# Attention and two feed-forward layers: token order inside a tile by residue mod 4, plain heads permuted in the matrix product, merged copies of x

## The chip, the cores and the metric

One core of a Trainium2 chip. The metric is the device time of one execution in microseconds (us), lower is better; for the kernel before it is the median of three runs.

## The reference

```python
# q, k, v: (4, 8, 576, 64) fp32; heads 0-3 "plain", heads 4-7 "dilated"
scores = q @ k.T / 8
rel = pos[:, None] - pos[None, :]
mask_plain = (rel >= 0) & (rel < 32)
mask_dil   = (rel >= 0) & (rel < 128) & (rel % 4 == 0)
attn = softmax(where(mask, scores, -1e9)) @ v            # per batch and head
x = attn.transpose(0, 2, 1, 3).reshape(2304, 512)         # tokens x model
x = (silu(x @ w_gate) * (x @ w_val)) @ w_out              # 512 -> 1536 -> 512
h = x @ w_in                                              # 512 -> 2048
return (h - tanh(h)) @ w_out2                             # 2048 -> 512, fp32
```

## The kernel before

The 2304 tokens are cut into six tiles of 384 (`TT`). The kernel holds x, the attention output, transposed: for a tile, two buffers of 128 partitions (two heads of 64 dimensions each) with a high and a low half in fp32r, `x[tile][kc][:, s, hp % 2, token]`, s = 0 for high and 1 for low. The feed-forward products then run in three passes over these halves (`up`, L543, the first layer before its sums exist; `product`, L554, with seven products in place of eight; `ffn1_out` L821 and `ffn2_out` L841).

Attention works in 48 units: a batch b (4), a pair of heads hp (hp 0 and 1 plain, 2 and 3 dilated) and a third g of the 576 queries, so 192 queries in three blocks of 64. For the dilated heads the host has sorted the 576 positions by residue mod 4, 144 of each residue in a row, so that their mask is the same band as that of the plain heads. A unit goes through these steps, each by one engine: load of q and k (SP queue, L472) and of v (L437); scores, three products (TensorE, L443); masked row maxima (VectorE, L448, three); exponentials with row sums (ScalarE, L454, three); 1 / sum (VectorE, L493 and L494, for one or two units together); normalisation (GpSimd, L458); three transposes (TensorE, L464); copy of the transposed weights `at` out of PSUM (VectorE L468 or ScalarE L470, in turn); the products with v, called mix here (TensorE, L510, moving operand `at`, stationary operand v, six per unit); and the copies of the result into x: high half by ScalarE (`put_hi`, L523), then the low half, PSUM minus high half, by VectorE (`put_lo`, L526).

`mixes` takes three units at a time, puts two of them in one PSUM bank and one in another, and makes one pair of copies per unit and piece. `spans` gives the pieces: a plain unit is 192 tokens in a row in one tile, so one piece of 192 columns. A dilated unit holds rows of one or two residues; its tokens lie in the tile at every fourth column, so each piece is written with a step of four fp32 elements (16 bytes), and a unit's piece is 48 or 96 columns long, since batches and tiles overlap (576 against 384).

The order of all work is made ahead of time by a planner written in the file (`Plan.order`): each task has an engine, an estimated duration, a priority and the ring buffers it needs; an engine takes the ready task of the lowest priority number. Attention units have priorities 0.3 apart in the order of `first_tile`; feed-forward tasks are put between them as their tiles of x and their weights become ready. Constants such as `KEEP_T`, `AHEAD` and `SECOND` bend this order. On the chip each engine then runs its list in order. Matrix weights come through the same SP queue and are converted from fp64 bits by ScalarE and VectorE (L332 to L345, L314, L317). The last stage of layer two adds up into `acc` (VectorE, L730) and stores 128 tokens at a time to the output (SP, L854).

Of the kernel before, what the change touches and what calls it, by code (L numbers as in the profile page):

```python
# [21 lines left out]
P = 128  # L22
# [235 lines left out]
def attention_then_two_ffns(ctx, tc, qk, vt, masks, w1, w2, out):  # L258
# [130 lines left out]
    x_done = [([], []) for _ in range(NT)]  # L389
    x_of = [[[] for _ in range(KC)] for _ in range(NT)]  # L390

    def spans(b, hp, g):

        base = b * S
        if hp < NP // 2:
            i, o = divmod(base + UT * g, TT)
            yield i, slice(0, UT), lambda xt, s: xt[:, s, hp % 2, o:o + UT]
            return
        cut = ((base // TT + 1) * TT - base) // DIL
        for r in range(DIL):  # L400
            for a0, a1 in ((0, cut), (cut, SA)):
                c0, c1 = max(r * SA + a0, g * UT), min(r * SA + a1, g * UT + UT)
                if c0 < c1:
                    i, o = divmod(base + DIL * (c0 - r * SA), TT)
                    yield (i, slice(c0 - g * UT, c1 - g * UT),
                           lambda xt, s, o=o, r=r, n=DIL * (c1 - c0): xt[:, s, hp % 2, o:o + n].rearrange(
                               "p (a f) -> p f a", f=DIL)[:, r, :])

    def idle(ps):

# [88 lines left out]
    def mixes(fronts, prio):  # L499

        banks = [new_ps() for _ in fronts[::2]]

        def mix():
            for j, (_, v, at, _) in enumerate(fronts):
                pv = banks[j // 2]
                covered[pv.slot] = 0
                for i in range(UN):
                    for h2 in range(2):
                        c, o = P * i + D * h2, j % 2 * UT + QT * i
                        nc.tensor.matmul(pv()[D * h2:D * h2 + D, o:o + QT],  # L510
                                         lhsT=v()[:KT, c:c + D], rhs=at()[:, c:c + D], start=True, stop=True)

        a = add_att("PE", 0.35 + 0.35 * len(fronts), prio, mix, [d for f in fronts for d in f[3]],
                    banks + [t for f in fronts for t in f[1:3]])
        a.fresh = idle(banks[0])
        for j, ((b, hp, g), _, _, _) in enumerate(fronts):
            pv = banks[j // 2]
            for i, cols, dst in spans(b, hp, g):
                n = cols.stop - cols.start
                cols = slice(j % 2 * UT + cols.start, j % 2 * UT + cols.stop)  # L520

                def put_hi(xt=x[i][hp // 2], cols=cols, dst=dst, pv=pv):
                    nc.scalar.activation(out=dst(xt(), 0), in_=pv()[:, cols], func=AF.Copy)  # L523

                def put_lo(xt=x[i][hp // 2], cols=cols, dst=dst, pv=pv):
                    nc.vector.tensor_tensor(out=dst(xt(), 1), in0=pv()[:, cols], in1=dst(xt(), 0).bitcast(F32),  # L526
                                            op=ALU.subtract)

                h = add_att("ACT", 0.05 + n / 1200 if n == UT else 0.035 + n / 850, prio, put_hi, [a], [pv, x[i][hp // 2]])
                x_of[i][hp].append(add_att("DVE", 0.07 + n / 960 if n == UT else 0.06 + n / 545, prio, put_lo, [h], [pv, x[i][hp // 2]]))  # L530
                x_done[i][hp // 2].append(x_of[i][hp][-1])

    covered = {}

# [296 lines left out]
    def ffn2_out(ws, ys, t, first, last, prio, end=False, early=None):  # L831
        pieces = []
        cuts = [(s, 0, DM) for s in range(NS)]
        if end:
            cuts[-1:] = [(NS - 1, 0, DM // 2), (NS - 1, DM // 2, DM)]
        for s, c0, c1 in cuts:
            def mm(ps, start=True, s=s, c0=c0, c1=c1):
                n = 0
                for w, y in zip(ws, ys):
                    for a, bb in PASSES:  # L840
                        nc.tensor.matmul(ps()[:, :c1 - c0], lhsT=y[0]()[:, a, s * P:(s + 1) * P],  # L841
                                         rhs=w[1][0]()[:, bb, c0:c1], start=(n == 0), stop=(n == 3 * len(ws) - 1))
                        n += 1
                covered[ps.slot] = c1 - c0

            pieces.append((mm, s * DM + c0, s * DM + c1, MM * 4 * len(ws) * (c1 - c0) / DM,
                           [d for _, d in ys] + [w[1][1] for w in ws], [w[1][0] for w in ws] + [y for y, _ in ys]))
        r = add_up(2, t, pieces, first, last, prio, early)
        if last:
            at, puts = r  # L850
            for (s, c0, c1), a in zip(cuts, puts):
                def store(s=s, c0=c0, c1=c1):
                    r0 = t * TT + s * P
                    nc.sync.dma_start(out=out[r0:r0 + P, c0:c1], in_=at()[:, s * DM + c0:s * DM + c1])  # L854

                plan.add("DMA", ISSUE, -1e6, store, [a], [at], work=0.9 * (c1 - c0) / DM)

# [105 lines left out]
    def first_tile(unit):  # L963
        b, hp, g = unit
        i = max(i for i, _, _ in spans(b, hp, g)) if hp < NP // 2 else b * S // TT
        return i, b, (hp < NP // 2) != PLAIN_FIRST, hp, g

    units = [(b, hp, g) for b in range(B) for hp in range(NP) for g in range(S // UT)]
    fronts, parts = [], []
    for n, unit in enumerate(sorted(units, key=first_tile)):  # L970
        prio = ATT0 + ATT_STEP * n
        if not parts:
            sm = new_sm()
        parts.append(attention(*unit, prio, ("DVE", "ACT")[n % 2], sm, len(parts)))
        many = FEW if n < SOON else TOGETHER
        if len(parts) == (1 if n < ALONE else ONE_SUM) or len(fronts) + len(parts) == many:
            fronts += inverted(parts, sm, prio - AHEAD)
            parts = []
        if len(fronts) == many:
            mixes(fronts, prio)  # L980
            fronts = []

    def given(*homes):
        got = {}
# [137 lines left out]
    def any_size():  # L1122
# [38 lines left out]

        for t in range(NT):
            xt = tile_of(t)
            rows = out[t * TT:(t + 1) * TT, :].rearrange("(s p) c -> p s c", p=P)
            for k in range(NK2):
                weights(wi, w2[k][:, :512])
                weights(wo, w2[k][:, 512:])
                h = ps[0][:, :TT]
                for kc in range(KC):
                    for n, (a, b) in enumerate(PASSES):  # L1170
                        nc.tensor.matmul(h, lhsT=wi[:, a, kc * P:(kc + 1) * P], rhs=xt[kc // 2][:, b, kc % 2, :],
                                         start=(kc == n == 0), stop=(kc == KC - 1 and n == 2))
                nc.scalar.activation(out=sq, in_=h, func=AF.Square)
                nc.scalar.activation(out=th, in_=h, func=AF.Tanh)
                nc.vector.scalar_tensor_tensor(out=g, in0=h, scalar=C2, in1=sq, op0=ALU.mult, op1=ALU.mult)
                nc.vector.tensor_tensor(out=th, in0=h, in1=th, op=ALU.subtract)
# [11 lines left out]
                part = at.rearrange("p (s c) -> p s c", s=NS)  # L1188
                if k == 0:
                    nc.sync.dma_start(out=rows, in_=part)  # L1190
                else:
                    nc.gpsimd.dma_start(out=rows, in_=part, accum_op=ALU.add)

    with tc.manual_schedule():
        for t in plan.order():
# [53 lines left out]
```

## Time and profile before

| | |
|---|---|
| median of three runs | 877.51 us (877.45 to 878.17) |
| the profiled execution, its own time | 877.31 us |
| its span, first to last instruction | 875.4 us |
| TensorE busy, share of the span | 863.8 us, 99% |
| VectorE | 722.1 us, 82% |
| ScalarE | 585.0 us, 67% |
| mean granted TensorE clock | 0.998 |

Time and span are of one execution; the 1.9 us between them lie outside the instructions. Matrix products are pipelined: a product's recorded duration reaches into the next one, so a TensorE that is busy all the time may still start its products later than it could. Every fp32 product stands in the trace as two records (288 for the 144 score products, 576 for the 288 mix products), every fp32r product as one.

### The profile page before, as it was taken

The numbers are of one execution on the slowest core, as the hardware profiler recorded it, in microseconds if no ns is written. First come the engines' busy times: TensorE is split into PE (matmuls) and PEld (weight loads), VectorE is DVE, ScalarE is ACT, GpSimd is POOL, SyncE is SP. The second block draws the span as 40 slices with busy tenths as digits, with TensorE's granted clock in tenths as the row PEclk, the third lists the DMA queues.
The fourth block names the chain that finished last, engine by engine and source line by source line (L and its number), as shares of the span: only waits on it lengthen the run. The fifth ranks groups of instructions, "written<-read, shape, count | busy, mean of one in ns | idle before, by whom it ended". The sixth has DMA issues, their size and how long they took to land.

```text
span 875.4 us, 15267 instructions
## 1 busy us (share of the span) xinstructions
PE 863.8 (99%) x5240; PEld 814.6 (93%) x5240; DVE 722.1 (82%) x1708; ACT 585.0 (67%) x1516; POOL 86.0 (10%) x116
## 2 busy tenths in 40 slices
PE   8999999999999999999999999999999999999996
PEld 6898999999999999999999999889989889898995
DVE  5999999989788788788759999978878777765675
ACT  6999757668667567668648887756666556564530
POOL 2333100000000000000000000011011010111100
PEclk9999999999999999999999999999999999999999
DMA  9997272583885885888895556899989796958995
GB/s 326 370 317 270 60 263 94 231 280 103 229 240 109 229 232 118 228 229 224 268 325 192 205 191 233 288 255 279 206 230 207 188 248 165 227 133 199 246 298 213
DMA packets 50455, 195.84 MB, mean 224 GB/s; under 512 B 5600, under 2 KB 12224, under 8 KB 50368
## 3 DMA queue, kind: packets, MB, share of 16 engines
q1 hardware_dynamic: 41728, 147.59, 47.0%
q0 software_dynamic: 8640, 47.19, 29.0%
q8 instruction: 43, 0.70, 0.3%
q14 instruction: 44, 0.36, 0.1%
HBM read 121.62 MB, written 73.14 MB: 222 GB/s over the span
## 4 chain that ended last, share of the span: by engine, by line
PE 88%; DVE 7%; DMA 1%; ACT 1%; issue 1%; POOL 0%; SPq 0%; POOLq 0%; DVEq 0%
PE ps L554 54%; PE ps L841 21%; PE ps L821 6%; PE ps L543 3%; PE ps L443 2%; PE ps L510 1%; DVE x L905 1%; DMA q<-qk 1%; PE ps L464 1%; DVE e L448 1%; DVE x L526 1%; DVE acc L920 1%; ACT e L454 1%; DVE t L701 0%; DVE t L698 0%
## 5 line engine op out<-in xcount | busy, mean ns | idle before, releaser
L554 PE MATMUL ps<-x,wc 128*128 128x384 f32 x2316 | 426.4, 336 | 0.0
L554 PEld LDWEIGHTS ps<-x,wc 128*128 128x128 f32 x2316 | 407.5, 188 | 4.4
L841 PE MATMUL ps<-wc,y 128*128 128x512 f32 (+1 forms) x870 | 208.9, 392 | 0.2 <-DVE t L701 0.2
L841 PEld LDWEIGHTS ps<-wc,y 128*128 128x128 f32 x870 | 161.9, 188 | 33.5 <-DVE t L701 0.6
L734 ACT ACTIVATE acc<-ps 128x512 f32<-128x512 f32 (+1 forms) x134 | 75.0, 560 | 77.4 <-PE ps L841 61.0
L761 POOL DMA_DIRECT2D sum<-acc x60 | 53.0, 883 | 678.4 <-ACT acc L734 273.2
L633 DVE TENSOR_TENSOR y<-t,y 128x384 fp32r<-128x384 f32 x168 | 92.4, 553 | 26.3 <-ACT y L630 26.0
L630 ACT ACTIVATE y<-t 128x384 fp32r<-128x384 f32 x168 | 86.4, 518 | 22.4 <-DVE t L701 8.4
L565 ACT ACTIVATE ps<-ps 128x384 f32<-128x384 f32 x156 | 73.7, 476 | 25.8 <-PE ps L554 22.1
L314 ACT ACTIVATE wc<-u 128x512 fp32r<-128x512 f32 x108 | 67.5, 631 | 26.6 <-PE ps L554 18.7
L317 DVE TENSOR_TENSOR wc<-u,wc 128x512 fp32r<-128x512 f32 x108 | 73.1, 684 | 3.7 <-ACT wc L314 2.4
L600 DVE TENSOR_TENSOR ps<-ps,t 128x384 f32<-128x384 f32 x56 | 31.5, 563 | 43.1 <-PE ps L554 43.1
L821 PE MATMUL ps<-y,wc 128*128 128x384 f32 x336 | 62.8, 337 | 0.0
L698 DVE SCALAR_TENSOR_TENSOR t<-t 128x384 f32<-128x384 f32 x96 | 52.7, 551 | 10.3 <-ACT t L695 9.5
L821 PEld LDWEIGHTS ps<-y,wc 128*128 128x128 f32 x336 | 58.8, 188 | 0.1
L454 ACT ACTIVATE e<-e,nm 128x96 f32<-128x96 f32 x144 | 52.1, 369 | 6.4 <-DVE nm L448 6.3
L695 ACT ACTIVATE t<-ps 128x384 f32<-128x384 f32 x72 | 34.9, 485 | 25.9 <-DVE ps L600 15.7
L332 ACT ACTIVATE u<-st 128x512 f32<-128x512 f32 x68 | 44.9, 666 | 9.0 <-DMA st<-w 8.7
L345 DVE SCALAR_TENSOR_TENSOR u<-st,u 128x512 uint32<-128x512 uint32 x68 | 46.8, 689 | 0.4
L340 DVE SCALAR_TENSOR_TENSOR u<-st,u 128x512 uint32<-128x512 uint32 x68 | 46.5, 684 | 0.7 <-DVE nm L448 0.2
L554 PE MATMUL ps<-y,wc 128*128 128x384 f32 x198 | 45.3, 336 | 0.0
L554 PE MATMUL ps<-ym,wm 128*128 128x384 f32 x198 | 43.0, 337 | 0.0
(87 smaller groups left out, 1077.2 us busy)
## 6 DMA issues: line engine op xcount, KB each, us to landing
x<-part SPq DMA_DIRECT2D x66, 768.0 KB, 7.2
sum<-acc POOLq DMA_DIRECT2D x60, 768.0 KB, 8.9
st<-w SPq DMA_DIRECT2D x68, 512.0 KB, 5.7
q<-qk SPq DMA_DIRECT2D x48, 304.0 KB, 5.4
sum<-acc SPq DMA_DIRECT2D x12, 768.0 KB, 5.8
part<-x SPq DMA_DIRECT2D x12, 768.0 KB, 3.4
acc<-sum SPq DMA_DIRECT2D x12, 768.0 KB, 7.5
v<-vt SPq DMA_DIRECT2D x47, 192.0 KB, 5.1
```

The source lines that it names most:

```text
L314: nc.scalar.activation(out=w()[:, 0, :], in_=u(), func=AF.Copy)
L317: nc.vector.tensor_tensor(out=w()[:, 1, :], in0=u(), in1=w()[:, 0, :].bitcast(F32), op=ALU.subtract)
L454: nc.scalar.activation(out=e()[:, i, :], in_=e()[:, i, :], func=AF.Exp, scale=-1.0, bias=nm()[:, i:i + 1], accum_out=sm()[:, sums.start + ...
L554: nc.tensor.matmul(ps()[:, :TT], lhsT=w()[:, i, c:c + P], rhs=rhs, start=(start and n == 0), stop=(n == 3 * len(cols) - 1), skip_group_che ...
L565: nc.scalar.activation(out=ps()[:, :TT], in_=src()[:, :TT], func=AF.Copy)
L630: nc.scalar.activation(out=y()[:, 0, :], in_=s(), func=AF.Copy)
L633: nc.vector.tensor_tensor(out=y()[:, 1, :], in0=s(), in1=y()[:, 0, :].bitcast(F32), op=ALU.subtract)
L698: nc.vector.scalar_tensor_tensor(out=sq(), in0=sq(), scalar=E0 / E1, in1=sq(), op0=ALU.add, op1=ALU.mult)
L734: nc.scalar.activation(out=o, in_=ps()[:, :c1 - c0], func=AF.Copy)
L761: nc.gpsimd.dma_start(out=keep, in_=at(), accum_op=ALU.add)
L821: nc.tensor.matmul(ps()[:, :TT], lhsT=w[2][0]()[:, a, m * P:(m + 1) * P], rhs=y[0]()[:, bb, :], start=(start and n == 0), stop=(n == 3 * l ...
L841: nc.tensor.matmul(ps()[:, :c1 - c0], lhsT=y[0]()[:, a, s * P:(s + 1) * P], rhs=w[1][0]()[:, bb, c0:c1], start=(n == 0), stop=(n == 3 * le ...
```

## The change

Inside a tile of 384 tokens, x is now held in the order of residue mod 4: 96 tokens of residue 0, 96 of residue 1, and so on. Nothing in the feed-forward layers depends on the order of the tokens in a tile.

- A dilated head's result already lies by residue, so its copies are now unbroken runs (`pieces`), and adjacent residues with the same range become one copy with two free dimensions (2x48 or 3x48).
- A plain head's tokens must be sorted. `mix` does it in the product: the moving operand `at` is read with a step of four elements, and the result is written to PSUM as four runs of 16 columns.
- Two plain units of one tile fill one bank of 384 columns and are copied by one high and one low copy of 384. The three dilated units of a batch and head pair form one set in two banks, and a copy may span two units.
- Units come in sets: for each tile the plain pairs of units, then the dilated sets of a batch that begins in it. From the second tile on, the two plain sets of a tile share one mix task of four units.
- The output stores undo the order: `rows_of` gives for each 128 rows of `acc` two runs of one residue, each stored to every fourth row of the output. 19 stores become 38. The fallback `any_size`, which is skipped in these runs, stores in the same way.
- Constants of the planner: `KEEP_T` 2 to 1, `AHEAD` 0 to 1, `SECOND` 2 to 6, and the estimated durations of the copies; `TOGETHER`, `FEW` and `SOON` go.

```diff
-LEAVE, KEEP_T = (5, 6), 2
+LEAVE, KEEP_T = (5, 6), 1
-TOGETHER, FEW, SOON = 3, 2, 0
+PAIRED = True
+EVAC = ("DVE", "ACT")
-ONE_SUM, ALONE, AHEAD = 2, 2, 0.0
-SECOND = 2.0
+ONE_SUM, ALONE, AHEAD = 2, 2, 1.0
+SECOND = 6
...
+    def pieces(b, hp, at, n):
+
         if hp < NP // 2:
+            yield tile_of_plain(b, at), 0, DIL, 0, AT, 0, AT
             return
...
+            for r0, r1, lo, hi in runs:
+                yield i, r0, r1, r0 * SA + lo - at, SA, b * SA + lo - i * AT, hi - lo
+
+    def rows_of(t, s):
+
+        rows = out.rearrange("(a r) c -> r a c", r=DIL)
         for r in range(DIL):
+            lo, hi = max(r * AT, s * P), min((r + 1) * AT, (s + 1) * P)
+            if lo < hi:
+                yield lo - s * P, hi - s * P, rows[r, t * AT + lo - r * AT:t * AT + hi - r * AT, :]
...
+                            to, src = pv()[D * h2:D * h2 + D, o:o + QT], at()[:, c:c + D]
+                            if hp < NP // 2:
+                                o = (b * SA + UT // DIL * g) % AT + QT // DIL * i
+                                to = pv()[D * h2:D * h2 + D, :TT].rearrange("p (r a) -> p r a", r=DIL)[:, :, o:o + QT // DIL]
+                                src = src.rearrange("k (a r) -> k r a", r=DIL)
+                            nc.tensor.matmul(to, lhsT=v()[:KT, c:c + D], rhs=src, start=True, stop=True)
...
+                        dst = xt[:, s, hp % 2, :].rearrange("p (r a) -> p r a", r=DIL)[:, r0:r0 + R, o:o + w]
+                        if R * w == TT:
+                            return xt[:, s, hp % 2, :], pv()[:, :TT]
+                        if R == 1:
+                            return dst[:, 0, :], pv()[:, c:c + w]
+                        src = pv()[:, c:c + R * step].rearrange("p (r a) -> p r a", a=step)
+                        return dst, src[:, :, :w]
...
                 def store(s=s, c0=c0, c1=c1):
-                    r0 = t * TT + s * P
-                    nc.sync.dma_start(out=out[r0:r0 + P, c0:c1], in_=at()[:, s * DM + c0:s * DM + c1])
+                    for p0, p1, rows in rows_of(t, s):
+                        nc.sync.dma_start(out=rows[:, c0:c1], in_=at()[p0:p1, s * DM + c0:s * DM + c1])
...
+    for i in range(NT):
+        for hp in range(NP // 2):
+            sets.append([(b, hp, g) for b, h, g in units if h == hp and tile_of_plain(b, g) == i])
+        for b in range(B):
+            if b * SA // AT == i:
+                sets += [[(b, hp, g) for g in range(S // UT)] for hp in range(NP // 2, NP)]
+    runs = []
+    for fronts in sets:
+        if runs and PAIRED and len(fronts) == 2 and len(runs[-1]) == 1 and len(runs[-1][0]) == 2 and len(runs) > 1:
+            runs[-1].append(fronts)
+        else:
+            runs.append([fronts])
```

**Low-half copies on VectorE.** VectorE's list before, where the second dilated mix of batch 0 is copied; x_452 and x_456 are the buffers of tiles 0 and 1, ps_507 and ps_520 the two banks of the mix. Nine copies for three units:

```order
L526 TENSOR_TENSOR x_456<-ps_507,x_456 128x48
L526 TENSOR_TENSOR x_452<-ps_507,x_452 128x96
L526 TENSOR_TENSOR x_456<-ps_507,x_456 128x48
L526 TENSOR_TENSOR x_452<-ps_507,x_452 128x96
L526 TENSOR_TENSOR x_456<-ps_507,x_456 128x48
L526 TENSOR_TENSOR x_452<-ps_507,x_452 128x48
L526 TENSOR_TENSOR x_452<-ps_520,x_452 128x48
L526 TENSOR_TENSOR x_456<-ps_520,x_456 128x48
L526 TENSOR_TENSOR x_452<-ps_520,x_452 128x96
L468 COPY at_618<-ps_576 96x384
```

The same place in the list of the changed kernel, where x_465 and x_469 are tiles 0 and 1 and ps_516 and ps_529 the banks:

```order
L561 TENSOR_TENSOR x_465<-ps_516,x_465 128x288
L561 TENSOR_TENSOR x_469<-ps_516,x_469 128x2x48
L561 TENSOR_TENSOR x_465<-ps_529,x_465 128x96
L561 TENSOR_TENSOR x_469<-ps_529,x_469 128x2x48
L510 TENSOR_SCALAR sm_541<-sm_541 128x6
L511 RECIPROCAL sm_541<-sm_541 128x6
```

Nine copies became four with the same number of elements, and all are unbroken in x. Over the whole list, 96 copies (24 of 192, 24 of 96, 48 of 48 columns) become 52 (12 of 384, 4 of 288, 4 of 192, 4 of 3x48, 8 of 2x48, 8 of 96, 12 of 48); ScalarE has the same high-half copies. The pairs of L493 and L494 fall from 33 to 29.

**Mix on TensorE.** TensorE's list before, around the second mix; the three units share two banks, and layer one's first products (L543) and the next transposes (L464) stand around it:

```order
L464 MATMUL ps_478<-ident,e_372 96x128 x3
L543 MATMUL ps_486<-x_350,wc_362 128x384 x6
L510 MATMUL ps_507<-at_450,v_218 64x64 x6
L510 MATMUL ps_507<-at_471,v_226 64x64 x6
L510 MATMUL ps_520<-at_503,v_334 64x64 x6
L464 MATMUL ps_543<-ident,e_385 96x128 x3
```

The changed kernel at the first mix task of four plain units (tile 1):

```order
L481 MATMUL ps_686<-ident,e_578 96x128 x3
L533 MATMUL ps_697<-at_545,v_368 64x4x16 x6
L533 MATMUL ps_697<-at_595,v_378 64x4x16 x6
L533 MATMUL ps_710<-at_650,v_452 64x4x16 x6
L533 MATMUL ps_710<-at_675,v_458 64x4x16 x6
L481 MATMUL ps_732<-ident,e_613 96x128 x3
```

The count of products is the same, 288 for all mixes; 144 of them now have the form 64x4x16. Up to the last mix, TensorE's list before holds 132 products of layer one (120 of L543, 12 of L821), and now 114 (102 and 12).

**Last stores on SP.** SP's list before, at the end (acc_9772 is the last tile's sum):

```order
L854 DMA out<-acc_9772 128x512 x2
L854 DMA out<-acc_9772 128x256 x2
L1197 COMPARE_AND_BRANCH
```

and now (acc_9674):

```order
L889 DMA out<-acc_9674 96x512
L889 DMA out<-acc_9674 32x512
L889 DMA out<-acc_9674 64x512 x2
L889 DMA out<-acc_9674 32x256
L889 DMA out<-acc_9674 96x256
L889 DMA out<-acc_9674 32x256
L889 DMA out<-acc_9674 96x256
L1244 COMPARE_AND_BRANCH
```

Each store became two, so two in place of one stand behind the last addition.

## Rows read from the trace of the kernel before

**Rows 1.** The page, busy time of each engine over the span.

```profile
PE 863.8 (99%) x5240; PEld 814.6 (93%) x5240; DVE 722.1 (82%) x1708; ACT 585.0 (67%) x1516; POOL 86.0 (10%) x116
```

**Rows 2.** Stretches: busy us (records) of PE, PEld, DVE, ACT, POOL; clock, DMA share, GB/s.

```profile
5.00:17.00 12.00, 10.50 (x78) 8.27 (x78) 7.51 (x57) 9.36 (x43) 3.90 (x6) 1.00 1.02 371
17.00:53.00 36.00, 35.08 (x460) 32.20 (x458) 34.89 (x211) 34.64 (x181) 12.01 (x18) 1.00 1.01 359
53.00:80.00 27.00, 26.22 (x331) 24.19 (x330) 26.52 (x153) 25.39 (x123) 10.36 (x16) 1.00 0.97 326
80.00:105.75 25.75, 25.75 (x289) 24.60 (x287) 25.44 (x105) 21.29 (x94) 6.02 (x9) 1.00 0.25 79
```

**Rows 3.** Chain of waits, 16-52 and 52-80 us: shares; pieces (start, length, count).

```profile
by line: DVE e L448 17.1%; DVE x L526 13.9%; ACT e L454 13.3%; DMA q<-qk 12.9%; issue 8.4%; DVE at L468 6.6%; POOL e L458 6.5%; DVE u L340 3.8%; DVE u L336 3.8%; ACT wc L314 3.2%; ACT x L523 2.7%; DVE sm L493 2.6%; DVE sm L494 2.5%; DVE u L
...
by line: PE ps L443 27.1%; PE ps L543 23.5%; PE ps L510 21.4%; PE ps L464 15.9%; DVE x L526 7.7%; DVE e L448 3.3%; issue 1.1%; DVE nm L448 0.7%
...
54.62 0.33 PE ps L464 x3
...
56.00 0.64 PE ps L443 x6
56.64 1.20 PE ps L510 x36
57.84 1.12 PE ps L464 x9
58.96 2.65 PE ps L443 x24
...
76.59 2.09 PE ps L543 x12
```

**Rows 4.** TensorE's groups from 17 to 105.75 us: records, busy us, mean ns, idle before.

```profile
L443 PE MATMUL ps<-q 128*128 128x96 f32 x240 | 30.7, 275 | 0.5 <-DMA q<-qk 0.5
L543 PE MATMUL ps<-x,wc 128*128 128x384 f32 x120 | 24.6, 346 | 0.2 <-DVE x L526 0.2
L510 PE MATMUL ps<-at,v 96*64 96x64 f32 x576 | 20.4, 225 | 0.0
L464 PE MATMUL ps<-ident,e 128*96 128x128 f32 x126 | 19.2, 277 | 1.0 <-DVE x L526 0.6 <-POOL e L458 0.2
L821 PE MATMUL ps<-y,wc 128*128 128x384 f32 x13 | 2.8, 350 | 0.0
```

**Rows 5.** Back-to-back copies of L526 on VectorE: stretch, its length, busy, records.

```profile
48.76:50.38 1.62, 1.62 (x9) 1.00 0.92 262
...
59.00:59.79 0.79, 0.79 (x3) 1.00 0.79 238
```

**Rows 6.** VectorE's groups by shape, 5 to 108 us, and L633 of the page.

```profile
L526 DVE TENSOR_TENSOR x<-ps,x 128x192 fp32r<-128x192 f32 x24 | 7.3, 346 | 0.0
...
L494 DVE RECIPROCAL sm<-sm 128x6 f32<-128x6 f32 x15 | 2.9, 192 | 0.5
...
L493 DVE TENSOR_SCALAR sm<-sm 128x6 f32<-128x6 f32 x15 | 2.5, 166 | 0.0
...
L633 DVE TENSOR_TENSOR y<-t,y 128x384 fp32r<-128x384 f32 x168 | 92.4, 553 | 26.3 <-ACT y L630 26.0
```

**Rows 7.** Back-to-back copies of L523 on ScalarE: stretch, its length, busy, records.

```profile
47.31:48.32 1.01, 1.01 (x9) 1.00 0.88 331
58.05:58.68 0.63, 0.63 (x3) 1.00 0.86 283
```

**Rows 8.** The last addition in the chain of waits, and the output stores' issue durations.

```profile
868.51 0.42 DVE acc L730
...
L854 SPq DMA_DIRECT2D out<-acc x19: 332/333/485, 838.3 to 869.0; - x19
```

**Rows 9.** TensorE's waits over the whole span: total us, times, longest.

```profile
PE ps L443 <- DMA q<-qk: 1.7, 2, 1.2
...
PE ps L464 <- DVE x L526: 0.6, 1, 0.6
```

More of the change, by code (lines that the diff above doesn't have):

```diff
@@ L497, in inverted, with mixes @@
         return [rest(a, p) for _, p, rest in parts]
-    def mixes(fronts, prio):
-        banks = [new_ps() for _ in fronts[::2]]
+    def mixes(sets, prio):
+        banks = [[new_ps() for _ in fronts[::2]] for fronts in sets]
         def mix():
[L504 to L511, printed above, removed]
-        a = add_att("PE", 0.35 + 0.35 * len(fronts), prio, mix, [d for f in fronts for d in f[3]],
[L514 to L531, printed above, removed]
@@ new lines, in mix @@
+            for fronts, pvs in zip(sets, banks):
+                for j, ((b, hp, g), v, at, _) in enumerate(fronts):
+                    pv = pvs[j // 2]
+                    covered[pv.slot] = 0
+                    for i in range(UN):
+                        for h2 in range(2):
+                            c, o = P * i + D * h2, j % 2 * UT + QT * i
+                            to, src = pv()[D * h2:D * h2 + D, o:o + QT], at()[:, c:c + D]
[4 more added lines that the diff above has]
+                            nc.tensor.matmul(to, lhsT=v()[:KT, c:c + D], rhs=src, start=True, stop=True)
@@ new lines, in mixes, with views, put_hi, put_lo @@
+        fronts = sum(sets, [])
+        a = add_att("PE", 0.35 + 0.35 * len(fronts), prio, mix, [d for f in fronts for d in f[3]],
+                    sum(banks, []) + [t for f in fronts for t in f[1:3]])
+        a.fresh = idle(banks[0][0])
+        for fronts, pvs in zip(sets, banks):
+            for j, pv in enumerate(pvs):
+                b, hp, g = fronts[0][0]
+                n = UT * len(fronts[2 * j:2 * j + 2])
+                for i, r0, r1, c, step, o, w in pieces(b, hp, g if hp < NP // 2 else 2 * UT * j, n):
+                    R, kc = r1 - r0, hp // 2
+                    def views(xt, s, hp=hp, r0=r0, R=R, o=o, w=w, pv=pv, c=c, step=step):
+                        dst = xt[:, s, hp % 2, :].rearrange("p (r a) -> p r a", r=DIL)[:, r0:r0 + R, o:o + w]
[5 more added lines that the diff above has]
+                        return dst, src[:, :, :w]
+                    def put_hi(xt=x[i][kc], views=views):
+                        dst, src = views(xt(), 0)
+                        nc.scalar.activation(out=dst, in_=src, func=AF.Copy)
+                    def put_lo(xt=x[i][kc], views=views):
+                        hi, src = views(xt(), 0)
+                        nc.vector.tensor_tensor(out=views(xt(), 1)[0], in0=src, in1=hi.bitcast(F32), op=ALU.subtract)
+                    m = R * w
+                    h = add_att("ACT", 0.05 + m / 1150, prio, put_hi, [a], [pv, x[i][kc]])
+                    x_of[i][hp].append(add_att("DVE", 0.07 + m / 960, prio, put_lo, [h], [pv, x[i][kc]]))
+                    x_done[i][kc].append(x_of[i][hp][-1])
@@ L962, in attention_then_two_ffns @@
     plan.add("PE", 0.43 * WARM, -1e6, warm_up, bufs=[ps_warm])
[L963 to L966, printed above, removed]
     units = [(b, hp, g) for b in range(B) for hp in range(NP) for g in range(S // UT)]
[L969 to L981, printed above, removed]
+    sets = []
+    for i in range(NT):
[4 more added lines that the diff above has]
+                sets += [[(b, hp, g) for g in range(S // UT)] for hp in range(NP // 2, NP)]
+    runs = []
+    for fronts in sets:
+        if runs and PAIRED and len(fronts) == 2 and len(runs[-1]) == 1 and len(runs[-1][0]) == 2 and len(runs) > 1:
+            runs[-1].append(fronts)
+        else:
+            runs.append([fronts])
+    n = 0
+    for run in runs:
+        done = []
+        for set_ in run:
+            fronts, parts = [], []
+            for unit in set_:
+                prio = ATT0 + ATT_STEP * n
+                if not parts:
+                    sm = new_sm()
+                parts.append(attention(*unit, prio, EVAC[n % len(EVAC)], sm, len(parts)))
+                if len(parts) == (1 if n < ALONE else ONE_SUM) or len(fronts) + len(parts) == len(set_):
+                    fronts += inverted(parts, sm, prio - AHEAD)
+                    parts = []
+                n += 1
+            done.append(fronts)
+        mixes(done, prio)
     def given(*homes):
@@ L1163, in any_size @@
             xt = tile_of(t)
-            rows = out[t * TT:(t + 1) * TT, :].rearrange("(s p) c -> p s c", p=P)
             for k in range(NK2):
@@ L1187, in any_size @@
                     nc.vector.tensor_copy(out=at[:, s * DM:(s + 1) * DM], in_=ps[1])
[L1188 to L1192, printed above, removed]
+                for s in range(NS):
+                    for p0, p1, rows in rows_of(t, s):
+                        part = at[p0:p1, s * DM:(s + 1) * DM]
+                        if k == 0:
+                            nc.sync.dma_start(out=rows, in_=part)
+                        else:
+                            nc.gpsimd.dma_start(out=rows, in_=part, accum_op=ALU.add)
     with tc.manual_schedule():
```

24 lines of the change are left out of this document (12 added, 12 removed).

## Prediction

> **What bounds the kernel now.** I read the page's busy shares first. TensorE is busy for 863.8 of 875.4 us, and no other engine reaches 85% [rows 1]. The change touches only attention, so the next view is the busy time in stretches up to the last mix, which ends near 105.75 us [rows 2]. From 80 us on TensorE is busy without a break, and it stays so to the end, as its 99% says. So the end moves by what TensorE loses less, or more, in its first hundred microseconds. In 17 to 80 us three engines are nearly full at once: TensorE 61.3, VectorE 61.4 and ScalarE 60.0 of 63 us, with a DMA share of 1.01 and 0.97 [rows 2].
>
> The chain of waits says who sets the pace there. Before 52 us it runs through VectorE (L448, L526, L468, L340, L336), ScalarE and loads. After 52 us the products hold 88% of it, and L526 is VectorE's largest share with 7.7% [rows 3].
>
> Since recorded products overlap, busy time hides late starts, and I count TensorE's work by its back-to-back pieces instead. A record of scores takes 0.64 / 6 = 0.107 us, of transposes 0.33 / 3 = 0.11, of the mix 1.20 / 36 = 0.033, of layer one 2.09 / 12 = 0.174 [rows 3]. From 17 to 105.75 us there are 240, 126, 576 and 133 of them [rows 4]: 25.7 + 13.9 + 19.2 + 23.1 = 81.9 us of 88.75. TensorE loses 6.8 us there. A part is the price of changing from one task to the next: nine transposes take 1.12 us against 3 x 0.33, so 0.04 a task; 24 score records 2.65 against 4 x 0.64, so 0.02 [rows 3]. For some 120 tasks that is 2.4 to 4.8 us. What is left, 2.0 to 4.4 us, is waiting, and the most that relief of the other engines can give back there.
>
> **What the change does, part by part.**
>
> *Low-half copies, VectorE.* Before: 72 dilated copies at 1.62 / 9 = 0.18 us and 24 plain ones at 0.79 / 3 = 0.263 [rows 5], 13.0 + 6.3 = 19.3 us. An unbroken copy costs 1.08 ns an element, by 553 against 346 ns for 384 and 192 columns [rows 6], and 0.263 - 192 x 0.00108 = 0.056 us fixed. After: 52 copies with the same 24 x 192 + 24 x 96 + 48 x 48 = 9216 elements, 52 x 0.056 + 9216 x 0.00108 = 2.9 + 10.0 = 12.9 us. VectorE saves 6.4 us.
>
> *Pairs of L493 and L494.* Four fewer, at most 0.166 + 0.192 us each [rows 6]: 1.4 us. Together 7.8 us, some 8% of VectorE's 94 us up to 105.75 [rows 2].
>
> *High-half copies, ScalarE.* Nine dilated ones (576 elements) take 1.01 us, three plain ones 0.63 [rows 7]. One price fits both rows: 0.063 us fixed and 0.76 ns an element. It gives 96 x 0.063 + 7.0 = 13.1 us before and 52 x 0.063 + 7.0 = 10.3 after: 2.8 us saved.
>
> *What of that reaches TensorE.* VectorE's load in 17 to 80 us falls from 97% to about 90%, and it stops leading the chain; TensorE then sets the pace earlier. Its own products are as many as before. The 18 products of layer one that now stand behind the last mix (18 x 0.174 = 3.1 us) are moved, not saved. The gain is therefore not the 7.8 us, but what TensorE waits less. Of the 2.0 to 4.4 us I take nearly the middle, 3.0: the direct waits that the trace names are short (0.6 us for L526, 1.7 us for q, over the whole span [rows 9]), and the rest are products placed late in the list because VectorE's list was long.
>
> *The permuted product.* 144 mix products, 288 records, 288 x 0.033 = 9.6 us, now read `at` with a step of 16 bytes. No row shows TensorE reading so. The nearest rows disagree. On VectorE a step of 16 bytes costs (1.62 - 9 x 0.056) / 576 = 1.94 ns an element against 1.08 unbroken [rows 5, 6], 1.8 times as much, but there both the high half's read and the low half's write have the step. On ScalarE, where the write alone has it, it costs nothing [rows 7]. So the product costs from 0 to 9.6 x 0.8 = 7.7 us more. I take 0 for the likeliest: two stepped accesses in 1.94 ns are 0.97 ns for one, and a product of the mix (two records, 64 columns) takes 2 x 0.033 us, 1.04 ns a column, so one stepped read would just keep up.
>
> [...]
>
> *Larger mix tasks.* Four units wait for the fourth's `at` before any of their products run. Behind such a task in TensorE's list stand transposes and scores, which then wait too. I cost it at nothing, since the planner puts ready tasks ahead of it; without that cover a task of 4 x 12 x 0.033 = 1.6 us comes late by up to one unit's step.
>
> *Planner's constants.* They reorder the start. TensorE's idle time in 5 to 17 us is 1.5 us [rows 2]: plus or minus 1.5, taken as 0.
>
> *Stores.* Behind the last addition (868.51 us, 0.42 long) stood one issue of about 0.33 us; now two [rows 8]. So 0.4 us more, between 0 (half the rows land sooner) and 0.7 (the pair before is in the way too). The other extra issues lie under TensorE's work.
>
> **Sum.** The profiled execution took 877.31 us, its span 875.4; the median of the runs is 877.51. Less 3.0, plus 0.4: 874.7 for such an execution, **874.9 us** against the median. With 2.0 to 4.4 us gained, 873.5 to 875.9.
>
> **Rivals.**
>
> *The stepped read slows TensorE (slower).* At VectorE's ratio the plain mixes cost 7.7 us more on the engine that sets the end: 877.5 - 3.0 + 0.4 + 7.7 = 882.6 us. For it: VectorE's rows, and that the mix is bound by its columns and so can hide nothing. Against it: ScalarE's. It cancels the gain at 2.6 us, 42 ns a record in place of 33, and makes the kernel slower by over 0.2% at 4.4 us, 49 ns. [...]
>
> *The waits are not VectorE's (no change).* In 17 to 80 us the DMA engines are as full as VectorE, and the attention's loads are not fewer. If TensorE only comes to wait for q, or ScalarE, at 95%, takes VectorE's place (it is relieved by 2.8 us, not 7.8), the gain shrinks to 0 to 1: 877 to 878 us. For it: loads hold 12.9% of the early chain [rows 3]. Against it: the waits for q are 1.7 us in all [rows 9].
>
> *All of it comes back.* 4.4 us of waiting and the 1.5 at the start: 877.5 - 5.9 + 0.4 = 872.0 us.
>
> **How the numbers follow.** The forecast has 0.45, the stepped read 0.25 (half of that at a part of its price, 878 to 881), no change 0.22, all back 0.08. What can be told from no change is 0.2%, 1.75 us, so faster is below 875.75 and slower above 879.25. Faster: most of the first case and all of the last, 0.50. Same: the rest of the first, most of the third and a little of the second, 0.28. Slower: 0.22. The range goes from 872.6, a gain of the size of the last case, to 881.5, most of the second; the likeliest case's own is 873.5 to 875.9.
>
> **What would show it.** Right: L526's 19.3 us back to back become about 13; nine copies of 0.18 become four; the plain mixes keep 0.033 us a record; the last mix comes some 6 us earlier (3.0 gained and 3.1 of layer one behind it); the chain after 30 us is TensorE's. Wrong: 24 plain records in more than 0.9 us; waits of L443 for q above 3 us; the chain before 52 us still VectorE's or ScalarE's; the end after the last addition longer by over 1 us.

## The result, and the profile after

The changed kernel takes 884.75 us (median of 6 runs, 883.70 to 885.72), the kernel before 877.48 beside it (876.29 to 878.40): ratio 1.0082, interval [1.0069, 1.0095]. It is 7.3 us slower, where 2.6 faster was forecast. The profiled execution took 883.7 us, its span is 881.9.

First the page, busy time of each engine, then the stretches of [rows 2]:

```profile
PE 869.7 (99%) x5238; PEld 821.5 (93%) x5239; DVE 714.7 (81%) x1656; ACT 583.2 (66%) x1472; POOL 85.4 (10%) x116
```

```profile
5.00:17.00 12.00, 10.74 (x89) 8.50 (x89) 6.18 (x48) 9.15 (x41) 3.89 (x6) 1.00 1.01 360
17.00:53.00 36.00, 35.91 (x434) 33.60 (x434) 34.03 (x210) 33.87 (x164) 12.67 (x20) 1.00 1.03 375
53.00:80.00 27.00, 27.00 (x321) 25.89 (x321) 23.09 (x127) 24.20 (x112) 8.95 (x13) 1.00 0.88 288
80.00:105.75 25.75, 25.75 (x282) 24.36 (x282) 24.23 (x94) 20.34 (x77) 6.65 (x10) 1.00 0.36 113
```

VectorE is relieved as forecast: 722.1 us busy became 714.7 [rows 1], and in 53 to 80 us 26.52 became 23.09 [rows 2]. TensorE has no break from 53 to 105.75 us. Yet it works 5.9 us more in all, with two records fewer than in [rows 1]. The chain of waits says in which line (L460 was L443, L481 L464, L533 L510, L561 L526, L578 L543); first its shares in 16 to 52 us, then those in 52 to 80 us, then pieces (start, length, count):

```profile
by line: PE ps L460 27.8%; PE ps L533 14.8%; PE ps L481 13.5%; DMA q<-qk 13.3%; DVE e L465 5.6%; DVE x L561 4.2%; PE ps L578 3.5%; issue 3.4%; DVE u L341 2.9%; DVE at L485 2.6%; POOL e L475 2.1%; DVE u L346 1.9%; DVE wc L318 1.2%; DVE u L33
```

```profile
by line: PE ps L460 35.0%; PE ps L533 29.5%; PE ps L578 19.2%; PE ps L481 17.1%
...
31.32 0.86 DVE x L561 x4
...
34.53 1.31 PE ps L460 x12
...
36.50 2.93 PE ps L533 x48
...
41.88 1.20 PE ps L533 x36
...
54.59 2.93 PE ps L533 x48
...
103.63 2.93 PE ps L533 x48
```

The 48 records of a mix of four plain units take 2.93 us, 0.061 a record. The dilated ones, which read unbroken, keep 1.20 / 36 = 0.033, as in [rows 3]. Nothing but TensorE is left in the chain from 34 to 105.75 us, and of VectorE's copies four stand back to back (0.86 us) where nine did in [rows 5]. The 288 plain records cost 288 x (0.061 - 0.033) = 8.1 us more, and the last mix ends at 106.6, later than the 105.75 of before. TensorE's wait for q, 1.7 us in [rows 9], is shorter:

```profile
PE ps L460 <- DMA q<-qk: 0.8, 2, 0.5
```

Then the end: the last addition, in the chain of waits, and the output stores on SP's queue, as in [rows 8]:

```profile
873.27 0.42 DVE acc L765
...
L889 SPq DMA_DIRECT2D out<-acc x38: 315/472/1343, 843.1 to 876.5; - x38
```

From the end of the last addition to that of the span it was 875.4 - 868.9 = 6.5 us [rows 8] and is now 881.9 - 873.7 = 8.2. The last store is issued 2.8 us behind that addition, before at once, and an issue takes 0.47 us in the median instead of 0.33, one 1.34. From 868.7 us on, 12 issues stand on the queue nearly without a break, and the last four start behind the addition:

```profile
L889 SPq DMA_DIRECT2D out<-acc x12: 316/524/1343, 868.7 to 876.5; - x12
```

### The profile page after: what moved, and what is told of

Read it like the earlier page. It is cut to its first block, busy times and chain, and to the rows that moved or that the text cites. A ratio compares the mean times of both kernels' runs of the same rounds, so it can differ in the third digit from the quotient of the medians.

```text
span 881.9 us, 15208 instructions
## 1 busy us (share of the span) xinstructions
PE 869.7 (99%) x5238; PEld 821.5 (93%) x5239; DVE 714.7 (81%) x1656; ACT 583.2 (66%) x1472; POOL 85.4 (10%) x116
## 4 chain that ended last, share of the span: by engine, by line
PE 86%; DVE 7%; DMA 4%; issue 1%; ACT 0%; SPq 0%; POOL 0%; POOLq 0%; DVEq 0%; ACTq 0%
PE ps L589 50%; PE ps L876 20%; PE ps L856 6%; PE ps L578 4%; PE ps L460 3%; PE ps L533 3%; DMA st<-w 2%; PE ps L481 2%; DMA q<-qk 1%; DVE x L940 1%; DVE acc L955 1%; DVE y L668 1%; DVE u L346 0%; DVE t L736 0%; DVE t L733 0%
```

## Experiments

Theory after the result: two prices, the read of `at` with a step of 16 bytes (about 8 us) and the stores cut in two (2 to 4 us), lie over a gain of the size forecast. Rivals: the price of the mix is that of PSUM written in four runs, not of the read; it is that of the new order of the units; there is no gain under the prices. Behind each time below stands its ratio to the kernel before, timed beside it, with the 95% interval.

**The read, the write, the step.** Plain heads are read unbroken:

```
-  src = src.rearrange("k (a r) -> k r a", r=DIL)
+  src = src.rearrange("k (r a) -> k r a", r=DIL)
```

> The changed kernel, but the mix of plain heads reads its weights in unbroken order; the four runs of 16 columns in PSUM stay. It leaves out the sorting of the plain heads' tokens, everything else is as in the change. If the stepped read is what costs (theory 1), a plain task of 48 records falls from 2.93 to about 1.6 us, and the time by 288 x 0.028 = 8 us less what TensorE then waits instead: 876 to 878.5 us. If the runs in PSUM cost (theory 2), the task stays near 2.9 us and the time near 884.7. If it is the order of the units and not the form of the product (theory 3), the records get shorter or not, but the time stays above 882.

Measured 876.18 us (11 runs), 0.9986 [0.9977, 0.9995] of before: 8.6 below the change. Its chain of waits shows the record back at 0.032:

```profile
35.04 1.55 PE ps L533 x48
39.03 1.20 PE ps L533 x36
```

The lists of all engines are the change's, so it is not their order that cost. The reverse, the read stepped and PSUM written in one run:

```
...
+  to = to.rearrange("p (r a) -> p r a", r=DIL)
```

> The changed kernel, but each plain product writes 64 columns of PSUM in one run, with the stepped read kept. It leaves out the placing of the four residues, so the plain heads' tokens are sorted only within 64. Theory 1 (stepped read): 48 records still take 2.9 us and the time stays at 884 to 886. Theory 2 (runs in PSUM): 1.6 us, and 876 to 878.5.

It takes 883.83 us, 1.0073 [1.0058, 1.0089], with 48 records in 2.93 us as in the change. The runs in PSUM account for at most 0.9 us (884.75 - 883.83 by the medians), and the records are no shorter without them; the read is the price. Then the same read with a step of two elements:

> The changed kernel, but the plain mix reads with a step of two elements, 8 bytes, and writes two runs of 32 in place; the tokens come out sorted by parity within 64 only. If any step other than one costs, 48 records take 2.9 us and the time stays at 884 to 886. If it is the 16 bytes (each element in another 16-byte piece), the step of 8 bytes costs half of it or nothing: 1.6 to 2.2 us, and 876 to 881.

It takes 876.63 us (10 runs), 0.9995 [0.9985, 1.0004]; its chain of waits:

```profile
52.02 1.55 PE ps L532 x48
...
97.27 1.56 PE ps L532 x48
```

The step of 8 bytes cost TensorE nothing (1.55 and 1.56 us for 48 records, 1.55 unbroken); the one of 16 nearly doubled the record (1.55 to 2.93). Other steps were not tried.

**The stores.** The 19 whole stores of before:

```
-  for p0, p1, rows in rows_of(t, s):
-      nc.sync.dma_start(out=rows[:, c0:c1], in_=at()[p0:p1, s * DM + c0:s * DM + c1])
+  r0 = t * TT + s * P
+  nc.sync.dma_start(out=out[r0:r0 + P, c0:c1], in_=at()[:, s * DM + c0:s * DM + c1])
```

> The changed kernel with the output stores of the kernel before: 128 rows at a time, 19 in place of 38. It leaves out the undoing of the order, so rows of the output stand in the order of residue. If the doubled stores hold up the end (theory: the SP queue falls behind the last additions), the time from the last addition to the end of the span falls from 8.2 to 6.5 us and the time by 1.7, to 883. If the end was longer for another reason, 884 to 885.5.

It takes 880.41 us, 1.0038 [1.0024, 1.0052]: 4.3 below the change, more than expected even after the result. The 19 stores have a median issue of 332 ns, and from the last addition to the end of the span it is 5.4 us instead of 8.2: it isn't one more issue that costs, but the 12 that stand on the queue at the end. Of the 3.8 us between the two profiled spans these 2.8 lie there; the last addition also ends 0.9 earlier (872.8 for 873.7), and why is not shown.

> The changed kernel, whole result; the second of each pair of stores of the last tile goes out on ScalarE's queue in place of SP's. If SP's issue rate holds up the end, the last store is issued close behind the last addition (873.7) and not at 876.5 us, and most of what whole stores gave (4.3 us) comes back: 881 to 882.5. If the number of stores or their stepped rows cost in the DMA engines and not in the queue, the time stays at 884 to 885.5. If ScalarE's wait for the addition holds up its own work, the last additions come later.

With the second store of each pair of the last tile on ScalarE's queue (`queue = nc.scalar if end and p0 else nc.sync`) it takes 884.89 us, 1.0083, and nothing is won. But SP's queue now waits for a transfer that it didn't wait for in the change:

```profile
SPq L890 <- DMA out<-acc: 4.2, 1, 4.2
```

So this run doesn't tell whether the issues on the queue or the transfers behind them hold up the end.

**A whole kernel without the stepped read.** Queries of plain blocks and their masks come in sorted in the inputs.

```
...
+  m = m.reshape(QT // DIL, DIL, KT).transpose(1, 0, 2).reshape(QT, KT)
+  plain = q[:, :H // 2].reshape(B, H // 2, S // QT, QT // DIL, DIL, D).transpose(0, 1, 2, 4, 3, 5)
...
```

> The changed kernel with the whole result kept, but the sorting of the plain heads moved to the host's layout: the 64 queries of a plain block arrive by residue, with two masks sorted alike (8 in place of 6), so the weights come out sorted and the mix reads unbroken, with the four runs in PSUM as in the change. If the stepped read alone made the product dear, the time is that of the kernel that read unbroken and left the sorting out, 876.2 us, plus at most 0.3 for two more masks in the first loads: 875.5 to 877. If the first masks' load or the order of loads matters more: 877 to 879.

> Host order and two store queues together, whole result. If the two costs are apart, the gains add up: 884.75 - 8.6 - 2 to 3 = 873 to 874.5 us, faster than the kernel before (877.4). If they share a cause, 875.5 to 877, as with host order alone.

> Host order, and the 19 whole stores of the kernel before; it leaves out the undoing of the order, so the output's rows stand by residue within a tile. It is what is left of the change when both costs are gone: 884.75 - 8.6 - 4.3 = 871.9 us, so 871 to 873, if they are apart: a gain of 5.5 us by the copies and the order of the units, where 3.0 were forecast. If the gain is the 3.0 of the forecast and one of the two effects was counted twice: 874 to 875.

They take 881.36, 881.84 and 877.90 us (the last 1.0006 [0.9997, 1.0015]). Between first and third the stores cost 3.5 again, but all three lie above the level expected if the two costs are apart, by 4.4 to 7.3 us. The larger mask load had changed the planner's order. TensorE's waits in the first show one that the change doesn't have, and in 86 to 91 us, where it ends, the granted clock is 0.66:

```profile
PE ps L483 <- DVE t L683: 2.2, 1, 2.2
...
86.00:91.00 5.00, 4.53 (x21) 3.92 (x21) 4.29 (x21) 3.20 (x14) 0.00 (x0) 0.66 0.55 197
```

To see the sorting without that order, the planner counts the load as before (`work=0.25 * (min(c1, 6) - c0)`), and every engine has the change's list:

> A whole kernel with the reference's result: the 64 queries of each plain block, and the masks of the plain kinds with them, come in sorted by residue in the inputs, so that the mix reads its weights unbroken. Against the run before of this kind, the planner now counts the mask load as the change does, and every engine has the same list of instructions in the same order as the change; only the mask load is half as large again. If the order of the lists made the wait of 2.2 us at line 483 in that run, it is gone here and the time is within 0.5 of the unsorted one with the unbroken read (876.2), 875.7 to 876.7, 48 records of 1.55 us. If the sorting itself (the masks) made it, the time stays at 881.

> The kernel above with the 19 whole stores of before; the undoing of the order at the stores is left out. It holds the change's copies and its order without either of its two costs. If the costs of the stepped read (8.6 us) and of the split stores (4.3) are apart and add up, the copies and the order gain 5.5 us on the kernel before: 871.9. If the forecast's 3.0 was right for the gain and the two costs overlap by 2.5, 874.4. If the copies were hidden anyway, no faster than before, 877 to 878.

The first takes 876.86 us (11 runs), 0.9997 [0.9988, 1.0006], 0.2 above the range expected: the wait of 2.2 us is gone, and so are 4.5 us that the other order had cost. The second takes 873.65, 0.9960 [0.9946, 0.9974]. It shows the gain under the prices, 3.6 us: between the gains of 3.0 and 5.5 that its expectation weighed, nearer 3.0. Its last mix and last addition, in the chain of waits:

```profile
98.42 1.55 PE ps L535 x48
...
865.54 0.42 DVE acc L767
```

The last mix ends at 100.0 instead of 105.75, the "some 6 us earlier" of the prediction, and the last addition stands 3.0 us ahead of [rows 8].

**What the gain is made of.** The twelve 384-wide low-half copies done twice:

```
+  times = 2 if R * w == TT else 1
...
+  for _ in range(times):
...
```

> The kernel above, and each of the twelve 384-wide low-half copies of x is issued a second time on VectorE (it writes the same values), which by the change's own rows gives VectorE back 12 x 0.47 = 5.6 us of the 6.4 that the merged copies took from it; the planner counts them. If the gain comes from a VectorE that is less busy, half or more of it is lost: 2.5 to 4 us over the kernel above. If it comes from ScalarE's merged copies, the order of the work or the new constants, the time stays within 1 us of it.

It takes 875.40 us (11 runs), 0.9977 [0.9965, 0.9988]: 1.75 of the 3.6 are lost, between the two expectations. But the planner counts the second copies, and every engine's list but GpSimd's has another order than in the kernel above. Another order alone cost 4.5 us above, so the 1.75 is not the price of 5.6 us of VectorE by itself; the last kernel of this section, whose lists are unchanged, is the cleaner measure. The planner's constants, alone and taken back (`KEEP_T`, `AHEAD`, `SECOND`):

> The kernel before with the three new constants of the planner (KEEP_T 1, AHEAD 1.0, SECOND 6) and nothing else of the change. If the constants make part of the 3.6 us, as the return of 5.6 us to VectorE leaves room for (it took back 1.75), it is 0.8 to 2 us faster than before: 875.2 to 876.5. If they serve only the new copies, it is within 1 us of before or slower: 876.5 to 879.

> The kernel with the unbroken read and whole stores (873.65, the undoing of the order left out), with the three constants of before. If the copies alone make the gain, it stays within 0.8 of 873.65. If the constants make part of it, 874.5 to 876. If the gain needs both (the order of before doesn't suit the new copies), 876 or more.

The constants alone take 881.44 us (878.87 to 882.80), 1.0041 [1.0025, 1.0057], a loss beyond what either case expected. The copies with the old constants take 876.29, 0.9989 [0.9979, 0.9998], 2.6 above the kernel with the new. Neither half gives the 3.6; the copies need the order that the new constants make, and that order doesn't suit the old copies. Where the first one loses, its timeline of TensorE and its stretches show:

```profile
81.83 0.38 PE L464 MATMUL ps<-ident,e 128*96 128x128 f32 x2
84.11 0.83 PE L464 MATMUL ps<-ident,e 128*96 128x128 f32 x6 [1.90 <-DVE x L526]
```

```profile
80.00:86.00 6.00, 4.10 (x77) 3.81 (x74) 5.86 (x19) 4.91 (x20) 1.57 (x2) 0.92 0.62 188
86.00:91.00 5.00, 5.00 (x50) 4.71 (x50) 4.28 (x25) 3.33 (x17) 0.00 (x0) 0.50 0.12 34
91.00:96.00 5.00, 5.00 (x23) 5.00 (x23) 3.46 (x25) 3.30 (x16) 1.96 (x3) 0.57 0.03 9
```

TensorE waits 1.9 us for the old copies of x (L526). Behind it, though it is busy all the time, its granted clock is 0.50 in 86 to 91 us and 0.57 in 91 to 96. The spread of the runs goes with it: those near 879 have a mean granted clock of 0.996, those above 882 of 0.992.

**Why the stores cost.** One store with steps of four rows instead of two, the order within each 128 tokens (`out.rearrange("(a r) c -> r a c", r=DIL)`); and two halves to unbroken rows (`for p0 in (0, P // 2)`):

> A whole kernel meant to keep the gain without the costs: queries of plain blocks and their masks sorted in the inputs as above, and the tokens of a tile in order of residue within each 128 instead of within all 384, so that each 128 rows of the result leave in one store (19 stores, whose rows in DRAM go by steps of 4) instead of two. The copies of x that cross a bound of 128 are split: 24 more small copies, about 1.3 us more on VectorE and 1.5 on ScalarE by the change's rows. If one store of many steps costs what a whole one costs, 871.9 plus 0 to 3: 872 to 875, below the kernel before. If the rows' steps and not the number of stores make the issue long, the last stores cost as in the change: 876 to 878.

> The kernel with the unbroken read and whole stores (873.65), the undoing of the order still left out, and each store cut into two by partitions 0 to 63 and 64 to 127, to unbroken rows in DRAM: 38 stores as in the change, without steps of 4 rows. If the number of stores costs, the last issue comes 3 to 3.5 us behind the last addition and the time is 876.5 to 877.2. If the steps of 4 rows make the issues long, these are 0.33 each, the last comes within 1 us, and the time is 873.7 to 874.5.

The first takes 899.68 us, 1.0258, far from what was expected: its last store is issued 16.8 us behind the last addition. The second takes 878.16 (11 runs), 4.5 above its whole stores. The stores on SP's queue, first of the one store by steps, then of the halves:

```profile
L897 SPq DMA_DIRECT2D out<-acc x19: 536/702/5592, 835.7 to 884.6; - x19
```

```profile
L892 SPq DMA_DIRECT2D out<-acc x38: 466/584/1350, 835.0 to 869.8; - x38
```

Halves without any step have the long issues of the change, and their last is issued 4.2 us behind the last addition. So cutting the stores costs by itself. One store that holds all four residues costs far more (one issue of 5.6 us). The step of four rows can't be its only reason, since the change's own stores have that step too, and their issues take 0.47 us in the median. What makes it so long stays open, and so does why the issue of 64 rows takes longer than that of 128.

**The order undone between the layers**, where x is copied from the sum of layer one, 21 copies on each engine (`dst.rearrange("p k (a r) -> p k r a", r=DIL)`):

> A whole kernel meant to keep the gain without the two costs. As in the kernel with the change's own lists, the queries of plain blocks and their masks come in sorted, so that the mix reads unbroken; the order of the tokens is undone between the two layers, where x is copied from the sum of the first: 21 copies on ScalarE and 21 subtractions on VectorE (842 and 948 ns each before) write with a step of 16 bytes, and the result leaves in the 19 whole stores of before. All lists stay as in that kernel. If a step of 16 bytes costs the two engines nothing, as it did the copies of x after the permuted product on ScalarE: 873.65 plus 0 to 0.6, below the kernel before. If it doubles there too as it did on TensorE, 18 to 20 us of work more on each engine behind the products, and 875 to 885.

It takes 887.96 us, 1.0123 [1.0107, 1.0139], beyond even the bad case. Its copies took 0.95 and 0.84 us in the kernel before; nine of the 30 on each engine still write unbroken, the shortest among them:

```profile
L945 DVE TENSOR_TENSOR x<-acc,x x30: 947/1559/1617, 111.2 to 550.1; 128x768 fp32r<-128x768 f32 x30
L942 ACT ACTIVATE x<-acc x30: 834/1584/1633, 109.4 to 548.4; 128x768 fp32r<-128x768 f32 x30
```

The step costs VectorE (1559 - 947) / 768 = 0.80 ns a column and ScalarE (1584 - 834) / 768 = 0.98. There it isn't hidden; the stretch from 465 to 505 us of this kernel, then of the one with whole stores and no undoing:

```profile
465.00:505.00 40.00, 34.15 (x180) 32.02 (x179) 39.90 (x54) 33.98 (x54) 0.00 (x0) 0.97 0.41 155
```

```profile
465.00:505.00 40.00, 40.00 (x224) 39.01 (x223) 39.76 (x69) 32.42 (x65) 0.00 (x0) 1.00 0.56 210
```

VectorE was already full between the layers (39.76 of 40 us), so its added time, 21 x 0.61 = 12.8 us, comes out nearly whole in the 14.3 us lost.

**The merged copies without the order of the tokens**, with the change's lists and constants:

```
-  dst = xt[:, s, hp % 2, :].rearrange("p (r a) -> p r a", r=DIL)[:, r0:r0 + R, o:o + w]
+  dst = xt[:, s, hp % 2, :].rearrange("p (a r) -> p r a", r=DIL)[:, r0:r0 + R, o:o + w]
-  src = src.rearrange("k (a r) -> k r a", r=DIL)
...
```

> A whole kernel with the inputs of before: the change's merged copies, its order of units, its lists and its constants, but the tokens of a tile stay in their natural order. The mix of plain heads reads and writes unbroken, the copies of dilated heads write with a step of 16 bytes as they did before, and the result leaves in 19 whole stores; neither of the change's two costs is there. Against the kernel with the change's lists and no cost (873.65), only the steps of the dilated copies are added: 12 x 192 columns on each engine at 0.8 to 0.9 ns a column (what the 21 copies between the layers paid for the same step), about 3.7 us more on VectorE and 4.3 on ScalarE. If VectorE's work is worth what 5.6 us of it cost (1.75), 874.5 to 876, below the kernel before. If the wait at 80 to 90 us that other orders showed comes back with the longer copies, 878 to 881.

It takes 875.32 us (11 runs), 0.9983 [0.9974, 0.9992]: a whole kernel, 1.8 us faster than before and 9.4 than the change, as expected. Its 288-wide dilated copies (L552, L556), then the unbroken ones of the kernel at 873.65 (L563, L559), groups by shape:

```profile
L552 ACT ACTIVATE x<-ps 128x288 fp32r<-128x288 f32 x4 | 2.7, 678 | 0.0
L556 DVE TENSOR_TENSOR x<-ps,x 128x288 fp32r<-128x288 f32 x4 | 2.7, 677 | 0.0
```

```profile
L563 DVE TENSOR_TENSOR x<-ps,x 128x288 fp32r<-128x288 f32 x4 | 1.8, 444 | 0.0
...
L559 ACT ACTIVATE x<-ps 128x288 fp32r<-128x288 f32 x4 | 1.6, 396 | 0.0
```

By the records' length the step costs (677 - 444) / 288 = 0.81 ns a column on VectorE and (678 - 396) / 288 = 0.98 on ScalarE, as between the layers. Records on ScalarE overlap (nine of 285 to 398 ns lie in the 1.01 us of [rows 7]), so here are also two stretches of four copies back to back, 576 columns as in [rows 7], first stepped, then unbroken:

```profile
23.88:24.86 0.98, 0.98 (x4) 1.00 1.04 389
```

```profile
24.70:25.38 0.68, 0.68 (x4) 1.00 1.02 389
```

By these the step costs ScalarE (0.98 - 0.68) / 576 = 0.5 ns a column. The plain mix, which writes PSUM in one run here, takes the same 1.55 us as with four runs of 16 columns; the runs cost the records nothing:

```profile
99.50 1.55 PE ps L528 x48
```

The pages of the two kernels, first this one, then that at 873.65:

```profile
PE 863.0 (99%) x5238; PEld 814.3 (93%) x5239; DVE 716.8 (82%) x1656; ACT 584.6 (67%) x1472; POOL 85.8 (10%) x116
```

```profile
PE 862.3 (99%) x5239; PEld 814.9 (93%) x5239; DVE 713.0 (82%) x1656; ACT 582.6 (67%) x1472; POOL 85.6 (10%) x116
```

All lists are the same, so the 1.7 us between the two medians are the price of the stepped copies, which keep VectorE busy for 3.8 us more and ScalarE for 2.0. The copies keep half of the gain (1.8 of 3.6) where the tokens stay in order.

## Why the prediction was wrong

The times before and after are joined by steps: before 877.25; the change's copies and lists without its prices 873.65 (-3.6); with its split stores alone added 876.86 (+3.2); with its stepped read 884.75 (+7.9), where the host no longer sorts the queries. By the other way round, from whole stores (880.41), the read is worth 6.8 and the stores 4.3: about one microsecond of the two overlaps.

- **The permuted product: the step that failed.** "I take 0 for the likeliest" was wrong; it costs 6.8 to 8.6 us, on both sides of the upper bound, 7.7. The sign named for it (24 plain records in more than 0.9 us) reads 2.93 / 2 = 1.46. Two arguments led there. One halved VectorE's 1.94 ns between two stepped accesses, so that one read takes 0.97 and keeps up with 1.04 ns a column; on TensorE the stepped read takes 0.061 / 32 = 1.9 ns a column by itself. The other read [rows 7] as "on ScalarE it costs nothing": with a fixed 0.063 us and 0.76 ns an element two unknowns were fitted to two rows under the assumption that a stepped element costs what an unbroken one does, which is what was to be found. That price gives 0.69 us for 576 columns in four copies. Unbroken they take 0.68, but stepped 0.98, hardly less than the nine copies of [rows 7] (1.01): for these it was the step and not their number that set the time. The rival at 882.6 us was the case; it falls 2.1 us short, mainly by the stores. In these runs a step of 16 bytes cost all three engines tried (0.9 ns a column on TensorE, 0.8 on VectorE, 0.5 to 0.98 on ScalarE), and on TensorE a step of 8 bytes cost nothing (1.55 us for 48 records, as unbroken).
- **Stores: mis-sized.** 0.4 us, with 0.7 as the bound, were 3.2 to 4.3. The prediction counted one more issue behind the last addition, and four start there. "The other extra issues lie under TensorE's work" failed: issues of 0.32 to 1.34 us pile up on SP's queue over the last additions, and what is left of the pile stands behind the last one. The end behind it is 1.7 us longer than before, where over 1 was the sign named, and 2.8 longer than with whole stores in the same kernel.
- **The gain: right in size.** 3.0 forecast, 3.6 measured (2.3 to 4.7 by the interval), with the last mix 6 us earlier. That the two numbers agree is partly luck, since 3.0 was about the middle of a range and the constants were taken as 0. The cause was told too simply: unbroken copies bear 1.7 of it at the same lists (the last kernel above), through both engines; the rest needs merged copies, order and constants together, which the runs don't part further.
- **Copies: right.** Nine became four, 1.62 us became 0.86 for 576 columns, the chain share of L526 in 52 to 80 us fell from [rows 3]'s 7.7% to none. ScalarE's price fits for unbroken copies (0.69 us forecast for four, 0.68 measured), though its page shows 1.8 us less busy where 2.8 were forecast.
- **Constants: 0 was right only in this company.** Alone they lose about 4 us; with the new copies they add 2.6 of the gain. A term of its own was the wrong form.
- **Larger mix tasks at nothing:** not tried alone, so it stays open; among TensorE's waits in the changed kernel none stands at the mix (L533).
- **The waits rival (no change)** fell: without the two prices the gain is there, and TensorE's wait for q fell from 1.7 us to 0.8 in the change.

## What to carry to other kernels

Ask of each access that a new layout steps: by how many bytes, and on which engine. Work moved into an operand of TensorE, which sets the end here, was free where the read was unbroken or stepped by 8 bytes (1.55 us for 48 records in both), and not where it stepped by 16 (2.93). A row that reads as "it costs nothing" must be compared with an unbroken row of the same shape before a bound rests on it. Count all stores of the last tiles as one queue: here, what they took beyond the time between additions stood behind the last one (the last store was issued 2.8 us behind the last addition). And a kernel that is meant to add a load to one engine must keep every list as it was, or it measures a new order as well.

## What the hardware showed unexpectedly

- The price of a 16-byte step was near the same on three engines: 0.9 ns a column on TensorE's read, and by the records' length 0.8 on VectorE (writes, and reads of the high half) and 0.98 on ScalarE's writes (0.5 in copies back to back). An 8-byte step cost TensorE nothing, and four runs of 16 columns in PSUM left its records as long as one run did (48 in 1.55 us each time).
- Issues on SP's queue were no constant: in the median 0.33 us for 128 whole rows, 0.58 for 64, 0.47 for the change's 32 to 96 rows by steps of four, and 0.70 for 128 rows of four residues in one store, with one of 5.6.
- A wait of TensorE of 1.9 us was followed by a granted clock of 0.50 in 86 to 91 us, and one of 2.2 us by 0.66 in the same stretch of another kernel. Each of these orders cost more than its wait (4.6 and 4.5 us).
